# Polysketch attention with a gated causal layer: 64-column projection tiles, per-head gate weights, zero matmuls and a new order

## The chip, the cores and the metric

The kernel runs on one core of one Trainium2 chip. A core has five engines that matter here: TensorE (PE, matrix products, with a row of its own for the loads of its stationary operand, PEld), VectorE (DVE), ScalarE (ACT), GpSimd (POOL) and SyncE (SP, which here only starts DMA transfers). Each engine works through its own instructions in the order in which they were issued, and waits on semaphores for the others. The metric is the device time of one execution in microseconds (us), as the median of the runs shown.

## The reference

With batch 4, 4 heads, sequence length 1088, head size 32 and sketch size r = 8, inputs and output in float32:

```python
def phi(x):                                   # S1, S2: 8 x 32
    a = einsum('rd,bhsd->bhsr', S1, x)
    b = einsum('rd,bhsd->bhsr', S2, x)
    return einsum('bhsi,bhsj->bhsij', a, b)   # 64 features for each row
q_p, k_p = phi(q), phi(k)
kv  = einsum('bhsf,bhsd->bhfd', k_p, v)       # over the whole sequence
z   = sum(k_p, axis=2)
num = einsum('bhsf,bhfd->bhsd', q_p, kv)
den = einsum('bhsf,bhf->bhs', q_p, z) + 1e-6
x   = (num / den) with the heads side by side # 4 x 1088 x 128
gate_pre[s] = sum over t<5 of conv_w[t] * x[s - 4 + t]
out = (sigmoid(gate_pre) * (x @ w_val)) @ w_out
```

The output of a batch needs the kv and z of the batch's whole sequence, so k and v of a batch come before the second half of its q.

## The kernel before

**Tiling.** A batch's sequence is cut into three units of twelve tiles of 32 rows (the last unit is padded). With four batches that makes twelve units for k and twelve for q, numbered 0 to 11. A unit of k or q is loaded as 128 partitions (4 heads x 32 rows) by 384 columns; a 32x32-block transpose on DVE (`kT`, `qT`, lines 293 and 432) brings the head dimension onto the partitions.

**k side.** `k_ab` (line 302) projects a unit on TensorE: for each of three column blocks t and each of four quarters x, one float32 matmul whose stationary operand is a 128x32 quarter of kT and whose moving operand is S3, the block-diagonal S1 and S2 (64 columns). It writes 32 partitions of PSUM: a tile of 128 rows by 32 columns of the array. `k_cp` copies the result to SBUF, `k_phi` multiplies out the 64 features (three per unit, on POOL, some on DVE), and `k_kv` (line 330) multiplies them with v, four float32 matmuls of 32 columns for each t. z is not summed from the features: `k_z` multiplies the two projections with each other, `z_mask` masks them on DVE, and `z_c` turns the result into a vector c that stands as a third block of 32 columns in the moving operand of the q projection (`rhsq`), so that a.c summed over i gives the denominator.

**From kv to weights.** The kernel doesn't compute x. It folds kv into the two following products. `kv_cols` (line 385) copies kv from PSUM into two masked copies side by side (128 columns, float32), `kv_bf` casts these to bf16, `wg_mm` (line 404) multiplies a 64-row half of them with `dcw`, the convolution weights on a diagonal (5 x 64 columns), `wg_ev` casts the result to the bf16 gate weights, and `kw_mm`, `kw_ev` make the value weights kw = kv @ w_val likewise.

**q side.** `q_ab` (line 437) projects a unit with the same quarters as k, 96 moving columns. `q_cp`, `q_prod`, `q_den`, `q_rc`, `q_an` make the denominator, its reciprocal and the normalised a; `q_phi` multiplies out the features in bf16 on DVE; `q_pt` transposes them on TensorE through the one PSUM buffer of tag "pt", and `q_ev` copies them to phiT. `q_halo` copies a batch's last tiles, shifted by one position, ahead of its first ones, so that the five taps find the rows before them.

**Output side.** Thirteen groups of up to 384 positions: `g_mm` (line 521, five taps for each of two head pairs, 64-column tiles) gives gate_pre, `g_sig` the sigmoid on ACT, `g_val` the values, `g_gv` their product (DVE or POOL), `g_out` the product with w_out, `g_ev` its copy, `g_st` the stores on SP (four to six DMAs for a group up to group 8, one for each later group; the last one on ACT).

**Buffers.** PSUM: one buffer of tag "k" (k projections from unit 3 on, half of the gate weights, the value weights, a few small ones), two of "q", one of "kv", one of "pt", three of "g" (the first three k projections, the other half of the gate weights, all of the output side). In SBUF there are two buffers for k and for v; q has one for all batches, so a q load waits for the transpose of the same unit of the batch before.

**Order.** The loads of k and q of batch 0, k and v of batch 1 and 0, the two weights and v of batch 1 are issued first, on SP. Then the setup: three zero matmuls into `warm_ps`, identities, masks, S3, with two more zero matmuls (lines 170 to 236). Everything after is a list written out in `ORDER` (line 637): each word is a step of the table `STEPS`, with its unit or batch, and a letter V, A or P ahead of the dot picks DVE, ACT or POOL in place of the step's usual engine in `HOME`. Every instruction is kept in that order on its engine. So where a step stands in the list decides what it queues behind on each engine that it uses, SP included.

All of the program's instructions carry the line of the helper that pins them (line 72), so the profile is read by the names of tiles: `abk` and `abq` are the projections' PSUM tiles, `ab_sb` and `ac` their copies, `phik` and `phiq` the features, `kv` the accumulators, `wg_ps` and `kw_ps` the weights, `pt` the transposed features, `g_ps`, `v_ps`, `o_ps` the output side.

Of the kernel before, what the change touches and what calls it, by code (L numbers as in the profile page):

```python
# [16 lines left out]
def kernel(  # L17
# [24 lines left out]
    B, H, S, D = q.shape  # L42
    r = S1.shape[0]
    assert (B, H, S, D, r) == (4, 4, 1088, 32, 8)
    P = 128
    R2 = r * r
    HR = H * r
    J, NT, U, M4, NCK = 32, 34, 3, 4, 3
    TU = M4 * NCK
    TM = U * NCK  # L50
    W = TU * J
# [26 lines left out]
    def ctile(shape, dt, name):  # L78
        return const.tile(shape, dt, tag=name, name=name)
# [139 lines left out]
    w_out_sb = ctile([P, P], BF16, "w_out_sb")  # L219

    id64 = ctile([P, 2 * D], F32, "id64")
    cwt = ctile([P, KT], F32, "cwt")
    dcw = ctile([P, KT, 2 * D], F32, "dcw")

    POOL.memset(w_val_sb, 0.0)
    POOL.memset(q_sb[0][:, NT * D :], 0.0)
# [7 lines left out]
        )  # L234
    POOL.tensor_copy(out=s2x, in_=S3[:, 1].unsqueeze(1).to_broadcast([P, NCK, HR]))
    POOL.tensor_tensor(out=id64, in0=identf[:, : 2 * D], in1=identf[:, 2 * D :], op=ALU.add)
    def conv_weights():
        cw_ps = ps_k.tile([P, KT], F32, tag="k", name="cw_ps")
        PE.transpose(cw_ps, cw_nat, identf[:KT, :KT])
        SCA.copy(out=cwt, in_=cw_ps)  # L240
        POOL.tensor_mul(
            dcw, id64.unsqueeze(1).to_broadcast([P, KT, 2 * D]),
            cwt.unsqueeze(2).to_broadcast([P, KT, 2 * D]),
        )

    def weights():
# [10 lines left out]
    def fill_2():  # L257
        for b in range(B):
            POOL.memset(phiT[b][:, :, 0].rearrange("p g (T j) -> p g T j", j=J)[:, :, :, 0:1], 0.0)

    def pad_k():

        POOL.memset(k_sb[0][:, NT * D :], 0.0)
# [4 lines left out]
    def s_rhs(eng, b):  # L268
        copy(eng, out=rhsq[b][:, 0:2, :], in_=S3)

    def s_chunks():
        s2_ps = ps_k.tile([NCK * HR, P], F32, tag="k", name="s2_ps")
        PE.transpose(s2_ps, s2x.rearrange("p t x -> p (t x)"), identf)
        SCA.copy(out=s2t, in_=s2_ps)

    kv_ps = [None] * B
    wg = [None] * B
    wgp, kwp, kvx, kvt, zms = ({} for _ in range(5))
    kw = [None] * B
    n_kv = [0] * B  # L280
# [4 lines left out]
    def copy(eng, out, in_):  # L285
        (eng.copy if eng is SCA else eng.tensor_copy)(out=out, in_=in_)

    def quarter(xT, u, t, x):
        lo = u * W + t * P + x * J
        return xT[:, lo : lo + J]  # L290


    def k_T(i):
# [8 lines left out]
    def k_ab(i):  # L302
        b, u = divmod(i, U)
        pool, tag = (ps_g, "g") if i < U else (ps_k, "k")
        ab = pool.tile([P, 2, NCK, HR], F32, tag=tag, name="abk")
        for t in range(NCK):
            for x in range(M4):
                PE.matmul(
                    ab[J * x : J * (x + 1), :, t, :], lhsT=quarter(kT[b], u, t, x), rhs=S3,
                    start=True, stop=True,  # L310
                )
        abk[i] = ab
# [62 lines left out]
    def z_c(eng, b):  # L375
# [6 lines left out]
            )  # L382
        copy(eng, out=rhsq[b][:, 2, :], in_=c_ps)

    def kv_cols(eng, b):

        kvx[b] = work.tile([P, 2, R2], F32, tag="kvx", name="kvx")
        if eng is SCA:
            for x in range(2):
                SCA.activation(  # L390
                    out=kvx[b][:, x], in_=kv_ps[b][:, :R2], func=ACT.Identity, scale=m2[:, x : x + 1]
                )
            return
        DVE.tensor_mul(
            kvx[b],
            kv_ps[b][:, :R2].unsqueeze(1).to_broadcast([P, 2, R2]),
            m2.unsqueeze(2).to_broadcast([P, 2, R2]),
        )

    def kv_bf(eng, b):  # L400
        kvt[b] = work.tile([P, P], BF16, tag="kvt", name="kvt")
        copy(eng, out=kvt[b], in_=kvx[b].rearrange("p x f -> p (x f)"))

    def wg_mm(b, g):
        gs = slice(2 * D * g, 2 * D * (g + 1))
        pool, tag = (ps_k, "k") if g == 0 else (ps_g, "g")
        wgp[b, g] = pool.tile([P, KT, 2 * D], F32, tag=tag, name="wg_ps")
        PE.matmul(
            wgp[b, g], lhsT=kvx[b].rearrange("p x f -> p (x f)")[gs], rhs=dcw[gs], start=True, stop=True
        )  # L410

    def wg_ev(eng, b, g):
        if wg[b] is None:
            wg[b] = work.tile([P, 2, KT, 2 * D], BF16, tag="wg", name="wg")
        copy(eng, out=wg[b][:, g], in_=wgp[b, g])

    def kw_mm(b):
        kwp[b] = ps_k.tile([P, 2, P], F32, tag="k", name="kw_ps")
        PE.matmul(kwp[b], lhsT=kvt[b], rhs=w_val_sb, start=True, stop=True)

    def kw_ev(eng, b):
        kw[b] = work.tile([P, 2, P], BF16, tag="kw", name="kw")
# [8 lines left out]
    def q_ab(i):  # L431
        b, u = q_unit(i)
        ab = ps_q.tile([P, 3, NCK, HR], F32, tag="q", name="abq")
        for t in range(NCK):
            for x in range(M4):
                PE.matmul(
                    ab[J * x : J * (x + 1), :, t, :], lhsT=quarter(qT[b], u, t, x), rhs=rhsq[b],
                    start=True, stop=True,
                )
        abq[i] = ab  # L440
# [169 lines left out]
    def g_st(i):  # L610
# [14 lines left out]
        ldk=load_k, ldq=load_q, ldv=load_v, pad=pad_k, f1=fill_1, f2=fill_2, w=weights,  # L625
        cw=conv_weights, mz=mask_z, sr=s_rhs, s2=s_chunks,
        kT=k_T, kab=k_ab, kcp=k_cp, kp=k_phi, kkv=k_kv, kz=k_z, zm=z_mask, c=z_c,
        kvx=kv_cols, kvt=kv_bf, wgm=wg_mm, wge=wg_ev, kwm=kw_mm, kwe=kw_ev,
        qT=q_T, qab=q_ab, qcp=q_cp, qpr=q_prod, qden=q_den, qrc=q_rc, qan=q_an, qphi=q_phi,
        qpt=q_pt, qev=q_ev, halo=q_halo,  # L630
        val=g_val, gmm=g_mm, sig=g_sig, gv=g_gv, o=g_out, oev=g_ev, st=g_st,
    )
    HOME = dict(
        {n: SCA for n in ("kcp", "c", "kvt", "wge", "kwe", "qcp", "qev", "oev")},
        **{n: POOL for n in ("sr", "kp", "qpr", "qan", "halo")}, kvx=DVE, gv=DVE,
    )
# [30 lines left out]
    for step in ORDER.split():
        name, *where = step.split(".")
# [31 lines left out]
```

## Time and profile before

| what | us |
|---|---|
| median of three runs | 65.04 |
| lowest and highest | 64.75, 65.14 |
| the profiled execution's own time | 64.56 |
| its span, first to last instruction | 62.8 |
| TensorE busy in the span | 52.3 |
| VectorE busy | 43.8 |
| ScalarE busy | 32.5 |
| GpSimd busy | 32.2 |

The profiled execution's time holds some 1.8 us outside its span. Two passes of TensorE make one float32 matmul, so each of them stands in the trace as two records. Records of TensorE are pipelined and their ends are modelled: the time that a group of matmuls takes is read from its first start to the next group's first start. In the timeline's lines a matmul is given with its rows and columns of the array (128*32) and its moving operand (128x64).

Further times of single operations, as the groups of the same profile give them: a phik product on POOL 626 ns, a phiq product on DVE 948 ns, a copy of pt on ACT 806 ns and on DVE 534 ns, a kT transpose 631 ns in the mean, a copy of a projection on ACT about 320 ns, a cast of the gate weights on ACT 429 ns, the memset of `zeros` on DVE 272 ns.

### The profile page before, as it was taken

Reading aid. Unit: us, or ns where it says so; the run is one execution under the profiler, and the core shown is the slowest. Engines: PE = TensorE matmul, PEld = TensorE weight load, DVE = VectorE, ACT = ScalarE, POOL = GpSimd, SP = SyncE. Lnnn points to the kernel's source line nnn. Section 1 sums busy time; section 2 is a strip of 40 time slices with the busy share of each in tenths; the row PEclk is TensorE's granted clock in tenths of the full one; section 3 lists DMA queues with packets and bytes.
Section 4 is the critical chain, followed back from the end, with each engine's and each line's share of the span. In section 5 each row is a group of like instructions: output and inputs, shape, how many; then the busy total and the mean of one; then the engine's idle time right before and its main releaser. Section 6 shows DMA issues by size and latency. Waiting matters only on the chain.

```text
span 62.8 us, 3063 instructions
## 1 busy us (share of the span) xinstructions
PE 52.3 (83%) x1269; PEld 37.5 (60%) x1269; DVE 43.8 (70%) x118; ACT 32.5 (52%) x85; POOL 32.2 (51%) x84
## 2 busy tenths in 40 slices
PE   1977958998994998999799999979999998986100
PEld 0215828986683596685677867748894675562000
DVE  2267968392979899995999995972793599837000
ACT  0823221324883329675748686353958757856200
POOL 5555368797895997629629992524630040000000
PEclk9999999999999999999999999999999999999996
DMA  0499995999701799898384311403023224402280
GB/s 0 71 336 345 365 297 152 259 241 318 247 25 24 189 262 258 284 266 220 108 243 124 86 31 33 120 15 83 22 63 89 63 52 118 110 23 72 94 257 16
DMA packets 9256, 9.38 MB, mean 149 GB/s; under 512 B 1941, under 2 KB 9242, under 8 KB 9242
## 3 DMA queue, kind: packets, MB, share of 16 engines
q1 hardware_dynamic: 9072, 9.05, 50.1%
q8 instruction: 10, 0.16, 1.1%
q10 hardware_dynamic: 170, 0.13, 0.7%
q14 instruction: 4, 0.03, 0.2%
HBM read 6.95 MB, written 2.23 MB: 146 GB/s over the span
## 4 chain that ended last, share of the span: by engine, by line
PE 42%; DMA 20%; DVE 19%; ACT 4%; SPq 3%; issue 3%; POOL 1%; DVEq 0%; ACTq 0%
PE g_ps L72 8%; DMA k_sb<-in_k_dram 7%; PE kv L72 7%; PE abq L72 7%; DMA v_sb<-in_v_dram 6%; PE abk L72 6%; DVE gv L72 5%; DVE phiq L72 4%; DMA q_sb<-in_q_dram 4%; PE warm_ps L72 4%; SPq L72 3%; PE o_ps L72 3%; DVE kT L72 2%; DMA out_dram<-o_sb 2%; DVE o_sb L72 2%
## 5 line engine op out<-in xcount | busy, mean ns | idle before, releaser
L72 POOL TENSOR_TENSOR phik<-ab_sb 128x256 f32<-128x256 f32 x32 | 19.4, 626 | 3.0 <-ACT ab_sb L72 2.8
L72 DVE TENSOR_TENSOR phiq<-an,abq 128x768 bf16<-128x768 f32 (+2 forms) x13 | 11.3, 886 | 0.4
L72 PE MATMUL g_ps<-phiT,wg 128*64 128x384 bf16 (+3 forms) x130 | 11.1, 308 | 0.2 <-DVE rden L72 0.2
L72 PE MATMUL abq<-rhsq,qT 128*32 128x96 f32 x288 | 8.9, 268 | 0.5 <-ACT rhsq L72 0.3
L72 DVE STREAM_TRANSPOSE kT<-k_sb 128x384 f32<-128x384 f32 x12 | 7.3, 631 | 2.2 <-DMA k_sb<-in_k_dram 2.2
L72 PE MATMUL abk<-S,kT 128*32 128x64 f32 x288 | 7.9, 255 | 1.0 <-DVE kw L72 0.8
L72 PEld LDWEIGHTS <-wg 128*64 128x64 bf16 x130 | 7.5, 109 | 1.8 <-issue 0.5
L72 DVE TENSOR_TENSOR gv<-gate,v_ps 128x256 bf16<-128x256 bf16 (+3 forms) x14 | 6.1, 453 | 3.4 <-PE v_ps L72 1.5
L72 ACT COPY phiT<-pt 128x768 bf16<-128x768 bf16 (+1 forms) x10 | 7.8, 784 | 1.0 <-PE pt L72 0.8
L72 ACT ACTIVATE gate<-g_ps 128x384 bf16<-128x384 f32 (+3 forms) x13 | 5.8, 451 | 4.9 <-PE g_ps L72 3.7
L72 PE MATMUL kv<-phik,v_sb 128*32 128x64 f32 x288 | 7.2, 234 | 0.8 <-DVE rhsq L72 0.4
L72 PEld LDWEIGHTS abq<-rhsq,qT 128*32 128x32 f32 x288 | 7.0, 120 | 1.0 <-ACT rhsq L72 0.4
L72 ACT COPY ab_sb<-abk 128x192 f32<-128x192 f32 x11 | 3.6, 323 | 7.1 <-PE abk L72 6.2
L72 POOL TENSOR_TENSOR prod<-ac 128x96 f32<-128x96 f32 x7 | 2.7, 390 | 8.7 <-ACT ac L72 7.9
L72 PEld LDWEIGHTS abk<-S,kT 128*32 128x32 f32 x288 | 6.0, 132 | 2.0 <-DVE kw L72 1.0
L72 PEld LDWEIGHTS kv<-phik,v_sb 128*32 128x32 f32 x288 | 5.7, 119 | 1.7 <-issue 1.1
L72 DVE STREAM_TRANSPOSE qT<-q_sb 128x384 f32<-128x384 f32 x12 | 6.5, 555 | 0.1
L72 PE MATMUL pt<-identity,phiq 128*128 128x128 bf16 x72 | 6.2, 220 | 0.0
L72 PE MATMUL v_ps<-phiT,kw 128*128 128x384 bf16 (+3 forms) x26 | 5.9, 308 | 0.0
L72 ACT COPY o_sb<-o_ps 128x384 f32<-128x384 f32 (+3 forms) x12 | 4.7, 411 | 1.9 <-PE o_ps L72 1.9
L72 PEld LDWEIGHTS <-phiq 128*128 128x128 bf16 x72 | 4.7, 98 | 1.1 <-issue 0.3
L72 PE MATMUL o_ps<-w_out_sb,gv 128*128 128x128 bf16 (+1 forms) x37 | 4.6, 224 | 0.8 <-DVE gv L72 0.6
(74 smaller groups left out, 64.4 us busy)
## 6 DMA issues: line engine op xcount, KB each, us to landing
v_sb<-in_v_dram SPq DMA_DIRECT2D x15, 144.0 KB, 3.6
q_sb<-in_q_dram SPq DMA_DIRECT2D x8, 192.0 KB, 3.7
k_sb<-in_k_dram SPq DMA_DIRECT2D x7, 192.0 KB, 3.9
out_dram<-o_sb SPq DMA_DIRECT2D x24, 48.0 KB, 1.6
q_sb<-in_q_dram SPq DMA_DIRECT2D x4, 160.0 KB, 3.3
k_sb<-in_k_dram SPq DMA_DIRECT2D x3, 160.0 KB, 4.0
k_sb<-in_k_dram SPq DMA_DIRECT2D x1, 384.0 KB, 3.4
out_dram<-o_sb SPq DMA_DIRECT2D x12, 32.0 KB, 1.6
```

The lines of the kernel that those rows point to most:

```text
L72: return lambda *a, **k: tc.keep_in_program_order(call(*a, **k))
```

## The change

1. The projections take halves in place of quarters: two matmuls for each t with a stationary operand of 128x64, each writing 64 partitions. The moving operands stay.
2. The gate weights: `kv_copy` copies kv once, unmasked, in float32 (step `kvx`, usually on ACT); `wg_mm` makes all four heads in one step, each head a matmul of 32 rows and 64 columns with 5 x 32 moving columns, written to its own half of the partitions. `wg_ev` copies each head's result onto its place in `wg`, which now exists once for each batch and whose other places are zeroed by the new step `f3` (two DVE memsets for each batch). The masked copy is made in bf16 from kvx by `kv_cols` (step `kvt`) and serves the value weights alone. `dcw` is half as wide, with a new 32-column identity `id32`.
3. A step `wm`: one zero matmul of 512 or 256 columns into `warm_ps`. Six of them stand in the list: two after s2, one after cw, one after kz.0, one after kz.2, one after c.0.
4. A new order. Up to the first kkv steps it is, on TensorE, s2, wm.0, wm.1, kab.0, cw, wm.2, kz.0, wm.3, kab.1, kab.2, kz.1, kz.2, wm.4, c.0, wm.5, qab.0, qab.1, kab.3. The memsets f3.3 and f3.1 stand ahead of kT.0, f3.0 and mz ahead of kT.1, and f3.2 later. Several copies change their engine (all qev and kwe are on ACT after; wge.2.0 and wge.3.0 on DVE).

```diff
-    dcw = ctile([P, KT, 2 * D], F32, "dcw")
+    dcw = ctile([P, KT, D], F32, "dcw")
+
+    wg = [ctile([P, 2, KT, 2 * D], BF16, f"wg{b}") for b in range(B)]
...
+    POOL.tensor_tensor(out=id32, in0=id64[:, :D], in1=id64[:, D:], op=ALU.add)
...
+    def fill_3(eng, b):
+        for x in range(2):
+            eng.memset(wg[b][R2 * x : R2 * (x + 1), :, :, D * (1 - x) : D * (2 - x)], 0.0)
...
+    def work_on_zeros(_, n):
+        PE.matmul(warm_ps[:, :n], lhsT=zeros[:, :P], rhs=zeros[:, :n], start=True, stop=True)
...
-    def quarter(xT, u, t, x):
-        lo = u * W + t * P + x * J
-        return xT[:, lo : lo + J]
+    def half(xT, u, t, x):
+        lo = u * W + t * P + x * 2 * J
+        return xT[:, lo : lo + 2 * J]
...
-            for x in range(M4):
+            for x in range(2):
                 PE.matmul(
-                    ab[J * x : J * (x + 1), :, t, :], lhsT=quarter(kT[b], u, t, x), rhs=S3,
+                    ab[2 * J * x : 2 * J * (x + 1), :, t, :], lhsT=half(kT[b], u, t, x), rhs=S3,
                     start=True, stop=True,
                 )
...
+    def kv_copy(eng, b):
+        kvx[b] = work.tile([P, R2], F32, tag="kvx", name="kvx")
+        copy(eng, out=kvx[b], in_=kv_ps[b][:, :R2])
...
+    def wg_mm(b):
+
+        for g in range(2):
+            pool, tag = (ps_k, "k") if g == 0 else (ps_g, "g")
+            wgp[b, g] = pool.tile([P, KT, D], F32, tag=tag, name="wg_ps")
+            for x in range(2):
+                hs = slice(D * (2 * g + x), D * (2 * g + x + 1))
+                PE.matmul(
+                    wgp[b, g][R2 * x : R2 * (x + 1)], lhsT=kvx[b][hs], rhs=dcw[hs], start=True, stop=True
                 )
...
     def wg_ev(eng, b, g):
-        if wg[b] is None:
-            wg[b] = work.tile([P, 2, KT, 2 * D], BF16, tag="wg", name="wg")
-        copy(eng, out=wg[b][:, g], in_=wgp[b, g])
+        for x in range(2):
+            xs = slice(R2 * x, R2 * (x + 1))
+            copy(eng, out=wg[b][xs, g, :, D * x : D * (x + 1)], in_=wgp[b, g][xs])
...
+    s2 wm.0.512 wm.1.512 f3.3 f3.1 pad f1 kT.0 f3.0 mz kab.0 kcp.0 cw wm.2.512 kz.0 wm.3.256 kT.1
+    sr.0 kT.2 kab.1 kab.2 kp.0.0 kcp.1 srA.1 kz.1 kcp.2 kz.2 wm.4.256 qT.1 qT.0 zm.0 c.0 wm.5.256
+    kpV.2.2 kpV.0.2 qab.0 qab.1 kT.3 kT.5 qcp.0 kp.1.1 kp.1.2 kab.3 f2 qcp.1 kkv.1.2 kpV.2.1 kT.4
...
+    kp.3.2 qprV.2 kz.3 wgm.0 kz.4 kkv.5.0 kkv.3.1 kz.5 kkv.4.0 ldq.5 zm.1 wge.0.0 wge.0.1 kkv.5.1
+    kkv.3.0 qden.2 c.1 kwm.0 kwe.0 kT.6 qrc.2 qpt.1 kp.4.1 qev.1 qab.3 halo.0 ldk.3 qcp.3 kab.6
...
+    qan.7 qrc.8 qan.8 o.3 kp.9.2 val.4 o.1 st.2 qpt.6 qT.10 oev.3 kz.10 kp.11.0 kp.11.2 qphi.7
+    kkv.10.1 kkv.9.0 oev.1 kz.11 qev.6 kkv.9.2 qphi.8 kp.11.1 kkv.11.2 st.3 kkv.10.2 kkv.10.0
+    kkv.11.0 zm.3 kkv.9.1 c.3 gv.4 qT.9 kkv.11.1 val.5 kvtP.2 qpt.7 qab.10 qab.9 o.4 gv.5 qev.7
+    qcp.9 kvxV.3 kwm.2 qcpV.10 qpr.10 haloV.2 qpt.8 oev.4 o.5 qprV.9 qev.8 oev.5 kwe.2 qden.10
+    qden.9 qrc.10 qT.11 gmm.6 gmm.8 sig.6 sig.8 gmm.7 qan.10 qrc.9 wgm.3 sig.7 kvtA.3 val.7 val.6
...
+    gv.10 qpt.11.1 qev.11.1 st.8 gv.9 o.10 gmm.11 val.11 oev.10 gmm.12 sig.11 val.12 gv.11 st.10 o.9
+    sig.12 gv.12 o.11 oev.9 st.9 o.12 oev.12 oevV.11 st.11 st.12
```

The list is cut. In the new list qT.2 stands behind qphi.0, which moves it past many DVE steps; kwe.0 stands on ACT ahead of kT.6; ldk.3 stands behind halo.0, and ldq.8, ldq.6 and ldv.2 follow it.

## The prediction

> **What bounds the kernel now.** I read the page first, then a table by stage, then the chain of waits, then TensorE's timeline.
>
> ```profile
> PE 52.3 (83%) x1269; PEld 37.5 (60%) x1269; DVE 43.8 (70%) x118; ACT 32.5 (52%) x85; POOL 32.2 (51%) x84
> ```
>
> The averages mix stages, so the stretches follow (span's start to 62.8 us; busy time of each engine, with instructions).
>
> ```profile
> 4.80:11.60 6.80, 5.43 (x153) 4.57 (x156) 5.02 (x11) 1.77 (x7) 4.12 (x8) 1.00 0.88 283
> 11.60:19.80 8.20, 7.17 (x248) 5.66 (x238) 6.13 (x17) 4.55 (x12) 7.31 (x21) 1.00 0.66 194
> 19.80:45.00 25.20, 24.26 (x727) 18.15 (x727) 21.17 (x58) 14.95 (x42) 16.71 (x33) 1.00 0.53 147
> 45.00:55.50 10.50, 10.01 (x126) 6.80 (x125) 8.32 (x22) 7.46 (x17) 1.39 (x4) 1.00 0.29 77
> ```
>
> From 19.8 on TensorE (first number) is busy 96% of the time and VectorE 84%; the others have room. Before that there are round trips and loads. Three pieces of the chain of waits:
>
> ```profile
> 9.41 0.20 ACT rhsq L72
> 9.65 1.23 PE abq L72 x24
> ...
> 13.12 4.61 DMA k_sb<-in_k_dram
> ```
>
> The q projection starts at 9.65, when a row of round trips (copy, z matmuls, mask, c) has ended. Batch 2 of k lands at 17.74; SP issues loads without a pause up to 11.65, so that landing does not follow the compute.
>
> TensorE's timeline (start, duration, instruction) gives the prices:
>
> ```profile
> 12.21 0.87 PE L72 MATMUL abk<-S,kT 128*32 128x64 f32 x24
> ...
> 19.79 0.54 PE L72 MATMUL abk<-S,kT 128*32 128x64 f32 x24 [0.79 <-DVE kw L72]
> 20.26 0.50 PE L72 MATMUL v_ps<-phiT,kw 128*128 128x384 bf16 x2
> 20.69 1.00 PE L72 MATMUL g_ps<-phiT,wg 128*64 128x384 bf16 x10
> ...
> 24.96 0.81 PE L72 MATMUL wg_ps<-dcw,kvx 64*128 64x320 f32 x4
> 25.70 0.34 PE L72 MATMUL o_ps<-w_out_sb,gv 128*128 128x128 bf16 x3
> ...
> 32.05 0.50 PE L72 MATMUL v_ps<-phiT,kw 128*128 128x384 bf16 x2
> 32.39 0.50 PE L72 MATMUL pt<-identity,phiq 128*128 128x128 bf16 x6
> ...
> 34.38 0.52 PE L72 MATMUL abk<-S,kT 128*32 128x64 f32 x24
> 34.72 0.86 PE L72 MATMUL kv<-phik,v_sb 128*32 128x64 f32 x32
> ...
> 37.11 0.68 PE L72 MATMUL abq<-rhsq,qT 128*32 128x96 f32 x24
> 37.64 0.54 PE L72 MATMUL abk<-S,kT 128*32 128x64 f32 x24
> ...
> 42.05 0.77 PE L72 MATMUL kv<-phik,v_sb 128*32 128x64 f32 x40 [0.41 <-DVE rhsq L72]
> ```
>
> A k projection lasts 0.34 us (34.38 to 34.72), a q projection some 0.52. At 12.21 the next kv matmuls follow at 12.85, so 0.64: the array runs at half speed there, and only after some 13.8 us at full speed. The granted clock reads 1.00 in both stretches, so it doesn't show this. Two v_ps take 0.34 when the same tile shape follows (32.05 to 32.39) and 0.43 when another follows (20.26 to 20.69): 0.09 us per change of tile shape.
>
> **64-column tiles.** The 24 records of a k projection are 12 matmuls in two passes, four tiles side by side: 6 slots of 56 ns. With 64 columns there are 12 records, two tiles side by side: 6 slots again. q likewise. I cost this at nothing, if two loads of 64 columns fit behind a slot. No row has that load. wg_ps bounds it: two passes of 320 columns at 56 ns per 64 are 0.56, the drain 0.09, and it holds TensorE 0.74 (24.96 to 25.70), which leaves 0.09 for a load of 128 columns, some 45 to 50 ns for 64. The other end is two loads one after the other, 100 ns. I take 50, since the kernel's four loads of 32 columns do run together. Behind a slot of 56 it is just hidden; after a change of shape it stands bare, some 25 ns more than with 32 columns, about 12 times: +0.3.
>
> **Changes of shape.** Here a rule speaks against the change: the Trainium skill, TensorEngine Tiling (Array Packing), Key Properties, says that changing the tiling mode, not just the tile, drains the engine. Projections and kv matmuls (both 32 columns now) no longer share a shape. It gives no price; the row does, 0.09. The rule taken with only the projections' shape changed in the old order, I count 25 more switches, +2.2 us. Counting along the two orders as given: 40 before, 53 after, by stage 1 to 10 up to the first kkv, 6 to 11 up to kab.6, 23 to 22 up to gmm.6, 10 and 10 after. So +0.9 in the front, +0.5 in the second stage, -0.1 in the long one.
>
> **Gate weights.** Now 0.107 at most of load and two passes, 0.65 without the drain. After: four tiles at once, two passes of 160 columns, 2 x 0.14 and 0.05 of load: 0.33. Four times -0.32. If pairs run one after the other the saving is nil; I take the four at once, as the present two row tiles run together. wge becomes two copies of 64x160 each: a 128x320 cast is 429 ns, 128x192 copies 319, so 290 each and some 0.1 more per wge where they follow closely. The masked ACT pair (0.52) becomes one kvx copy (some 0.2) ahead of wgm; kvt falls off that path. POOL loses three kvt at 0.29; the half-width dcw saves about 0.3 there, id32 costs 0.2.
>
> **Front.** f3.3, f3.1 are four memsets ahead of kT.0. The zeros row is 272 ns for 256 words; these have 320 bf16, 160 words: 0.17 each, 0.33 if done by element. 0.7 to 1.3 in all; I take 0.7, the zeros row being in words. kT.0 then starts at about 4.1 instead of 3.9, kab.0 at 5.0 (4.82). cw and wm.2 (0.43 at half speed) and two drains put kz.0 at 6.5 (6.12); wm.3 and two more drains, kab.1 at 7.1 (6.25). Behind it wait kcp.1, kcp.2, zm, c and both q projections: qab at 10.3 (9.65), first kkv, with kab.3 moved ahead of it, at 12.9 (11.57): +0.7 like for like at half speed.
>
> Against that stands the clock. The Trainium skill, TensorE: Matmul & The Clock Gate, Part 1, says about 3.4 us of sustained activity in a free-running window releases the full rate. By that rule, with fillers from 4.0 on, release would come near 7.5 and give back kab.1 and kab.2 (0.7), both qab (0.9) and the kv and k work up to 13.8 (1.0). The row is less kind: in this run 7.0 to 10.4 was about 58% streaming and released nothing; 10.4 to 13.8, about 91%, did. With fillers I count some 80% from 3.6 to 7.0, then 61%. No run shows whether 80% is enough. Ends: nothing, or 2.5; I take release about 10.4, worth 1.2, so the front nets -0.5.
>
> **Up to kab.6.** kab.6 starts at 19.79, after 0.95 idle behind kweV.0, queued on DVE behind kT.6 and kT.7. After, kwe.0 is on ACT ahead of kT.6. From first kkv: 14 kkv 1.6, two each of kab, qab, qpt 2.4, small steps 0.9, eleven drains with loads 1.3: 6.2, so 18.5 to 19.6; the landing at 17.74 plus kT.6 (0.57) allows 18.4 at the earliest. I take 19.1: -0.7, which contains the front's part. SP: ldq.5 now waits for the later qT.2, with ldk.3, ldq.8, ldq.6 and ldv.2 queued behind it; the DMAs were idle from 17.3 to 20.4, so that is covered to about 17.
>
> **kab.6 to gmm.6.** 25.2 before. Five kkv now lie earlier (-0.56), two wgm -0.64, drains -0.1, bare loads +0.3. The waits after c (30.48 and 42.05, 0.5 to 0.6 each), where kkv followed c at once: after c.1 and c.2 other work follows, after c.3 not: -0.5. DVE loses two qev, kwe, an oev and three kp (about 4.0) and gains f3.2, copies and products (about 1.5); ACT gains some 2.3 (60% to 73%), POOL some 1.3. With these queues denser, new waits of 0 to 1.5: I take 0.7, half, as no row tells. Sum -0.8.
>
> **Tail.** gmm.6 onward is nearly the same: wgm.3 -0.32; o.9, for which gmm.11 waited 0.4, goes behind val.12. But SP issues 24 stores of 0.42 us almost without pause from 45 to 57.9, and the last three behind them. I take -0.2.
>
> Sum: -0.7 - 0.8 - 0.2 = -1.7. The profiled execution took 64.56 (span 62.8 and 1.8 around it), so 62.9; the median shown is 0.48 above it: **63.3 us**.
>
> **Rivals and chances.**
> (a) Forecast, 62.3 to 64.3: 0.49.
> (b) Release near 7 us and no new waits: -0.6 more at kab.6 (stopped by the landing), -0.7 in the long stage: 62.0. For it the 80%. 0.13.
> (c) The fillers do not do what they are for and the waits are at their upper end: +0.5 and +0.8 on (a): 64.6, no change. 0.16.
> (d) Slower: loads of two 64-column tiles don't run together. A slot becomes 100 instead of 56 for k and 83 for q: 72 x 44 + 72 x 17 ns = 4.4 us, minus 1.7: 67.7. It decides from a slot of 80 (72 x 24 = 1.7). Against it: today's loads overlap. 0.08.
> (e) Slower: the window falls badly. TensorE works without gaps from some 10.3; with a free window of 3.4 us the release can come as late as two windows on, 17.1, and half of 6.8 us, 3.4, is lost against (a). kab.6 then starts near 21.8 instead of 19.1: 66.0. It decides from kab.6 at 20.8. Against it: the runs shown lie within 0.4 us of each other, though the window would fall anew in each. 0.14.
>
> About 1% is what this kernel's measurement can tell from no change: 64.4 to 65.7. Faster 0.62, which is (a) and (b); same 0.16, (c); slower 0.22, (d) and (e). The range 61.3 to 66.4 takes in the middle of (b) and (e) and leaves out (d), half of (e)'s upper side and the edge of (b): under 2 in 10.
>
> **What would show it.** wg_ps near 0.42 from its start to the next matmul; abk still 0.34 from 12 records; abk at half speed only before about 10.4; kab.6 near 19.1; gmm.6 near 43. It is wrong if abk's slots exceed 56 ns, if kab.1 is later than 7.5 while the array stays slow to 13.8, or if new idle before pt, abk and kv in 19 to 43 is over 1.5 us.

## The result, and the profile after

The changed kernel took 62.05 us in the median of four executions (61.43 to 63.13), against 64.90 (64.70 to 65.14) before, next to it on the same chip: a ratio of 0.948, with a 95% interval of 0.941 to 0.954. The forecast was 63.3. Faster was right, but the gain is some 2.85 us where 1.7 were forecast. The profiled execution took 61.57 us with a span of 59.9. (All ratios in this text leave out executions more than 1.5% above their kernel's fastest.)

The page of the changed kernel: first the engines' busy time, then the queue that fetches instructions (packets, MB, share), then the shares of the chain of waits.

```profile
PE 50.7 (85%) x1003; PEld 36.2 (60%) x1003; DVE 44.3 (74%) x127; ACT 34.7 (58%) x96; POOL 31.8 (53%) x81
...
q8 instruction: 8, 0.13, 0.9%
...
PE 60%; DVE 15%; ACT 8%; issue 4%; POOL 4%; DVEq 0%; ACTq 0%
```

Before, the last of these lines read

```profile
PE 42%; DMA 20%; DVE 19%; ACT 4%; SPq 3%; issue 3%; POOL 1%; DVEq 0%; ACTq 0%
```

The loads, a fifth of the chain before, are gone from it, and TensorE has gone from 42% to 60%. The prediction did not ask for that; the last experiments below bear on where it comes from.

The table by stage, with the stages cut at the same steps as before (first kkv at 11.2, kab.6 at 17.9, gmm.6 at 42.5):

```profile
4.80:11.20 6.40, 5.77 (x106) 4.14 (x105) 5.54 (x15) 1.79 (x8) 4.58 (x17) 1.00 0.95 312
11.20:17.90 6.70, 6.39 (x212) 5.14 (x211) 5.95 (x19) 4.74 (x16) 6.58 (x15) 1.00 0.92 268
17.90:42.50 24.60, 23.10 (x543) 17.88 (x539) 20.37 (x57) 16.59 (x45) 16.54 (x31) 1.00 0.47 137
```

| stretch, us | before | after | difference | forecast |
|---|---|---|---|---|
| start to kab.6 | 19.8 | 17.9 | -1.85 | -0.7 |
| kab.6 to gmm.6 | 25.2 | 24.6 | -0.6 | -0.8 |
| gmm.6 to the end | 17.8 | 17.3 | -0.4 | -0.2 |

So it is the stretch before kab.6 that was missed. TensorE's timeline after (start, duration, instruction, records) shows why:

```profile
5.19 0.91 PE L72 MATMUL abk<-S,kT 128*64 128x64 f32 x12 [0.19 <-DVE kT L72]
6.03 0.27 PE L72 MATMUL cw_ps<-identf,cw_nat 5*128 5x5 f32 x1
6.23 0.59 PE L72 MATMUL warm_ps<-zeros 128*128 128x512 bf16 x1
6.74 0.27 PE L72 MATMUL kv<-ab_sb 128*32 128x1 f32 x8
6.94 0.28 PE L72 MATMUL warm_ps<-zeros 128*128 128x256 bf16 x1
7.16 0.92 PE L72 MATMUL abk<-S,kT 128*64 128x64 f32 x24
...
9.74 1.21 PE L72 MATMUL abq<-rhsq,qT 128*64 128x96 f32 x24 [0.18 <-ACT rhsq L72]
10.75 0.55 PE L72 MATMUL abk<-S,kT 128*64 128x64 f32 x12
11.22 0.54 PE L72 MATMUL kv<-phik,v_sb 128*32 128x64 f32 x24
```

kab.0 at 5.19 takes 0.91, half speed. kab.1 and kab.2 together, 24 records from 7.16, take 0.92: full speed. The array's clock was released in between: the trace's own clock record has full rate from 6.66 on, some 7 us earlier than before (13.82), and both q projections take 1.0 us instead of 1.9. The forecast had put the release at 10.4.

### The profile page after: what moved, and what is told of

It reads as the page before. It is cut to its first block, busy times and chain, and to the rows that moved or that the text cites. A ratio compares the mean times of both kernels' runs of the same rounds, so it can differ in the third digit from the quotient of the medians.

```text
span 59.9 us, 2553 instructions
## 1 busy us (share of the span) xinstructions
PE 50.7 (85%) x1003; PEld 36.2 (60%) x1003; DVE 44.3 (74%) x127; ACT 34.7 (58%) x96; POOL 31.8 (53%) x81
## 4 chain that ended last, share of the span: by engine, by line
PE 60%; DVE 15%; ACT 8%; issue 4%; POOL 4%; DVEq 0%; ACTq 0%
PE kv L72 12%; PE g_ps L72 11%; PE abq L72 10%; PE abk L72 7%; PE v_ps L72 5%; PE pt L72 5%; PE warm_ps L72 4%; DVE gv L72 4%; DVE wg L72 3%; POOL phik L72 3%; PE wg_ps L72 2%; PE o_ps L72 2%; DVE o_sb L72 2%; ACT wg L72 2%; DVE kT L72 1%
## 5 line engine op out<-in xcount | busy, mean ns | idle before, releaser
L72 POOL TENSOR_TENSOR phik<-ab_sb 128x256 f32<-128x256 f32 x33 | 19.9, 629 | 0.3 <-ACT ab_sb L72 0.3
L72 DVE TENSOR_TENSOR phiq<-an,abq 128x768 bf16<-128x768 f32 (+2 forms) x13 | 11.2, 881 | 0.1
L72 ACT COPY phiT<-pt 128x768 bf16<-128x768 bf16 (+2 forms) x13 | 9.7, 753 | 1.9 <-PE pt L72 1.7
L72 PE MATMUL abq<-rhsq,qT 128*64 128x96 f32 x144 | 7.7, 251 | 0.2 <-ACT rhsq L72 0.2
L72 PE MATMUL kv<-phik,v_sb 128*32 128x64 f32 x288 | 6.7, 223 | 1.1 <-DVE zm L72 0.6
L72 PE MATMUL abk<-S,kT 128*64 128x64 f32 x144 | 6.8, 234 | 0.2 <-DVE kT L72 0.2
L72 PEld LDWEIGHTS abq<-rhsq,qT 128*64 128x64 f32 x144 | 6.3, 136 | 0.8 <-POOL phiT L72 0.3
L72 PEld LDWEIGHTS abk<-S,kT 128*64 128x64 f32 x144 | 5.6, 144 | 1.7 <-DVE kT L72 1.1
L72 PE MATMUL warm_ps<-zeros 128*128 128x512 bf16 (+1 forms) x11 | 5.0, 529 | 1.3 <-DVE hm L72 1.3
L72 PEld LDWEIGHTS kv<-phik,v_sb 128*32 128x32 f32 x288 | 4.8, 109 | 2.1 <-DVE zm L72 0.9
```

The costliest lines, as they stand in the source:

```text
L72: return lambda *a, **k: tc.keep_in_program_order(call(*a, **k))
```

## Experiments

Besides the ratios, each kernel's profile gives the start of four steps; "full" is the release, where the clock record of the trace begins to read full rate. All times in us, one execution for each line.

| kernel | zero matmuls | full | first kkv | kab.6 | gmm.6 | span |
|---|---|---|---|---|---|---|
| before | 0 | 13.8 | 11.6 | 19.8 | 45.0 | 62.8 |
| changed kernel | 6 | 6.7 | 11.2 | 17.9 | 42.5 | 59.9 |
| changed, again (e5) | 6 | 4.9 | 11.3 | 18.4 | 42.6 | 60.2 |
| changed, third time (e9) | 6 | 14.1 | 13.5 | 20.2 | 44.5 | 61.4 |
| changed, first two zeros only (e10) | 2 | 14.1 | 13.1 | 20.0 | 44.3 | 62.3 |
| changed, no zeros (e1) | 0 | 15.9 | 13.1 | 20.8 | 45.0 | 62.7 |
| changed, 32 columns (e4) | 6 | 5.5 | 11.0 | 18.7 | 44.7 | 62.0 |
| changed, 32 columns again (e11) | 6 | 4.7 | 11.3 | 21.4 | 46.7 | 64.6 |
| old order, zeros (e2) | 6 | 5.0 | 10.6 | 19.9 | 45.6 | 63.5 |
| old order, 64 columns (e3) | 0 | 15.4 | 11.9 | 20.3 | 46.5 | 64.2 |
| old order, new gate weights (e6) | 0 | 13.1 | 11.5 | 19.6 | 48.0 | 65.6 |
| old order, zeros, kwe.0 on ScalarE (e7) | 6 | 7.6 | 10.8 | 18.8 | 46.6 | 64.4 |
| old order, zeros, 64 columns, kwe.0 on ScalarE (e12) | 6 | 5.8 | 10.8 | 17.8 | 44.8 | 61.6 |
| changed, order moved again (e8) | 7 | 7.1 | 11.3 | 18.2 | 42.6 | 60.6 |

### The zero matmuls

Theory A: the gain before kab.6 is the early release. The rival: it comes from the new order and the 64-column tiles.

**e1: the changed kernel without its zero matmuls.**

```diff
-    s2 wm.0.512 wm.1.512 f3.3 f3.1 pad f1 kT.0 f3.0 mz kab.0 kcp.0 cw wm.2.512 kz.0 wm.3.256 kT.1
-    sr.0 kT.2 kab.1 kab.2 kp.0.0 kcp.1 srA.1 kz.1 kcp.2 kz.2 wm.4.256 qT.1 qT.0 zm.0 c.0 wm.5.256
+    s2 f3.3 f3.1 pad f1 kT.0 f3.0 mz kab.0 kcp.0 cw kz.0 kT.1
+    sr.0 kT.2 kab.1 kab.2 kp.0.0 kcp.1 srA.1 kz.1 kcp.2 kz.2 qT.1 qT.0 zm.0 c.0
```

> The changed kernel without its six zero matmuls (wm steps left out of the order, nothing else; the result is the same). Theory A (the gain over the forecast comes from the array reaching full speed near 7.2 instead of 13.8 us, and the zero matmuls bring that): kab.1 and kab.2 run at half speed (a k projection 0.64 and not 0.35), full speed only somewhere between 10.4 and 14, and the time is 0.8 to 2.0 us above the changed kernel's 61.5. Theory B (the gain is the order's; the front is covered by the loads of batch 2): within 0.3 us of 61.5 either way, kab.6 still near 18.

64.23 us (63.04 to 64.45); before on that chip 65.71 (64.47 to 67.78). The timeline of e1 has the same steps at half speed:

```profile
6.83 1.70 PE L72 MATMUL abk<-S,kT 128*64 128x64 f32 x24
...
10.30 2.19 PE L72 MATMUL abq<-rhsq,qT 128*64 128x96 f32 x24 [0.40 <-ACT rhsq L72]
12.24 0.89 PE L72 MATMUL abk<-S,kT 128*64 128x64 f32 x12
13.06 0.87 PE L72 MATMUL kv<-phik,v_sb 128*32 128x64 f32 x24
```

Full speed comes at 15.9 and kab.6 at 20.8, 2.8 after the changed kernel's and 1.0 after the old one's. So the whole gain before kab.6 hangs on the early release, which is missing without the zeros. But the time stays below the kernel before, so the rest of the change does bring something, later.

**e2: the old order with the six zero matmuls**, at places like those of the changed kernel.

```diff
-    s2 f1 kT.0 cw kT.1 kab.0 srA.0 kcp.0 pad kz.0 kab.1 kT.2 kab.2 mz qT.1 kcp.1 qT.2 kcp.2 kp.0.2
-    kp.2.0 qT.0 kz.1 kz.2 zm.0 c.0 qab.1 kp.1.2 kp.2.2 kp.1.1 qab.0 kkv.1.2 qcp.1 ldq.3 qpr.1
+    s2 wm.0.512 wm.1.512 f1 kT.0 cw kT.1 kab.0 wm.2.512 srA.0 kcp.0 pad kz.0 wm.3.256 kab.1 kT.2 kab.2 mz qT.1 kcp.1 qT.2 kcp.2 kp.0.2
+    kp.2.0 qT.0 kz.1 kz.2 wm.4.256 zm.0 c.0 wm.5.256 qab.1 kp.1.2 kp.2.2 kp.1.1 qab.0 kkv.1.2 qcp.1 ldq.3 qpr.1
```

> The kernel before with the six zero matmuls at the corresponding places of its own order (two after s2, one each after kab.0, kz.0, kz.2 and c.0). Theory A: full speed by 7 to 11 us, and 0.8 to 1.6 us faster than before (63.3 to 64.1), less than that if kab.6 still waits for kweV.0 and the k load at 17.7. Theory B: the same as before or up to 0.4 slower, since two matmuls of 0.43 push kab.0 back by about 0.35.

65.44 us (64.49 to 67.84), ratio 0.995 (0.987 to 1.003): no change. Yet the release came at 5.0, and kkv started 1.0 earlier. The timeline of e2 shows where that went:

```profile
10.59 0.28 PE L72 MATMUL kv<-phik,v_sb 128*32 128x64 f32 x2
11.87 0.31 PE L72 MATMUL kv<-phik,v_sb 128*32 128x64 f32 x4 [1.01 <-DMA v_sb<-in_v_dram]
```

TensorE, now early, stands for v, and again at kab.6 for kw (1.0 us, kweV.0 in VectorE's queue, as before the change). In the old order an early clock alone is worth nothing that these runs can tell.

**e5 and e9: the changed kernel again, on two chips; e10: it with the first two zero matmuls only.**

```diff
-    s2 wm.0.512 wm.1.512 f3.3 f3.1 pad f1 kT.0 f3.0 mz kab.0 kcp.0 cw wm.2.512 kz.0 wm.3.256 kT.1
-    sr.0 kT.2 kab.1 kab.2 kp.0.0 kcp.1 srA.1 kz.1 kcp.2 kz.2 wm.4.256 qT.1 qT.0 zm.0 c.0 wm.5.256
+    s2 wm.0.512 wm.1.512 f3.3 f3.1 pad f1 kT.0 f3.0 mz kab.0 kcp.0 cw kz.0 kT.1
+    sr.0 kT.2 kab.1 kab.2 kp.0.0 kcp.1 srA.1 kz.1 kcp.2 kz.2 qT.1 qT.0 zm.0 c.0
```

> The changed kernel itself, to stand beside the other runs on one chip. Earlier runs: without its zero matmuls 62.7 us span (kab.6 at 20.8), with 32-column tiles 62.0 (kab.6 at 18.7). If both parts are needed, this run has kab.6 near 18, gmm.6 near 42.5, a span near 60, and no halt of TensorE over 0.4 us that has no wait behind it. If the earlier differences were the chip's, the span is 62 or more here.

> The changed kernel once more, so that the three others stand beside it on one chip. Both theories expect 62 to 62.6 us and a ratio to the kernel before of 0.95 to 0.96. Theory A (the gain sits in an early release of the clock, and the new order and the 64-column tiles let what follows use it) expects full speed from between 5.2 and 7.2, first kkv near 11.3, kab.6 near 18.0 to 18.4 and gmm.6 near 42.6.

> The changed kernel with the first two of the six zero matmuls (3.94 to 5.0 in its trace) and without the four later ones; the result is the same. If what counts is the stretch up to some 5.2, which in this form is filled as before, full speed comes by 5.2 and the time is that of the changed kernel within 0.5 us (62 to 63). If the later ones are needed, because the stretch that counts can fall on 5 to 9, full speed comes as late as in the changed kernel without any (15.9), kab.6 starts near 20.7 and the time is some 64.5. If it depends on where a window falls in an execution, single times scatter between these two, by 2 us or more.

e5: 63.13 us (61.97 to 64.17) against 65.05, ratio 0.959 (0.953 to 0.965). e9: 62.75 (62.02 to 63.77) against 65.76, ratio 0.953 (0.941 to 0.966). e10, on e9's chip: 63.81 (63.35 to 64.24), ratio 0.978 (0.967 to 0.988). The profiled execution of e9 took 63.13 us. Its timeline:

```profile
6.24 0.61 PE L72 MATMUL warm_ps<-zeros 128*128 128x512 bf16 x1
6.77 0.34 PE L72 MATMUL kv<-ab_sb 128*32 128x1 f32 x8
7.04 0.39 PE L72 MATMUL warm_ps<-zeros 128*128 128x256 bf16 x1
7.37 1.55 PE L72 MATMUL abk<-S,kT 128*64 128x64 f32 x24
...
10.69 2.19 PE L72 MATMUL abq<-rhsq,qT 128*64 128x96 f32 x24
12.64 0.88 PE L72 MATMUL abk<-S,kT 128*64 128x64 f32 x12
13.45 0.84 PE L72 MATMUL kv<-phik,v_sb 128*32 128x64 f32 x24
14.23 0.57 PE L72 MATMUL abk<-S,kT 128*64 128x64 f32 x12
```

Up to 6.2 this execution is the same as the first profile to 0.02 us, with the same zeros, and then the release does not come: it comes at 14.1. In all profiles, with zeros or without, it fell at 4.7 to 7.6 or at 13.1 to 15.9, and never between. With at least six zeros it was early in eight of nine profiles; with none or two, late in five of five. The 14 executions of the changed kernel lie between 61.4 and 64.2 (median 62.7); e5 (61.97 us) and the first profile (61.57 us) are early, e9 late, so a late release fits much of that scatter, though only three of the 14 were profiled.

**What decides.** The clock records of the traces show it. They begin at the release, which is why the stage tables print 1.00 ahead of it as well. In each of the 14 profiles every stretch at full rate lasts a whole number of steps of 3.413 us: 51.20 us in the first profile is 15 of them, 44.37 in e9 is 13. So the clock changes only at the end of such a step, and counting back from the release tells where the steps of an execution lie. They lie differently each time: one ended at 6.66 in the first profile, at 7.31 in e9. From the starts and columns of the matmul records I estimate in what share of each step TensorE was streaming (at half rate 512 columns of zeros take 0.43 us in these traces). In every step that ended with a release it was at least 75%; in every step at half rate that ended without one, at most 70%. The first profile's step up to 6.66 has 77%. In e9 the steps that end at 7.31 and 10.72 have 69% and 63%, and the one that ends at 14.13 has 95%.

Slid along e9's trace, a step finds its 71 to 75% early, by some 7.0, in 76 to 87 of 100 positions and otherwise only at 13.6 to 14.4. In e10's trace it does so early in 41 to 58 of 100, in e1's and in the kernel before in none. (These are estimates, from one trace each.) So six zeros make an early release likely, not certain. e10's profile can't show that the first two zeros are too few: its steps lay as e9's did (14.12 and 14.13), where six didn't do either.

Two sizes follow. On one chip, the four later zeros take the median from 63.81 to 62.75, of a gain of 3.0 in all, and the ratio from 0.978 to 0.953: a third to a half of the gain. Each of these medians mixes early and late releases in a share that isn't known. The rest is there with a release at 14.1: e10's profile has kab.6 at 20.0, no earlier than before, but only 24.3 us from there to gmm.6 in place of 25.2, and e1's has the same 24.3.

### The 64-column tiles

Theory A: they cost nothing, as forecast. The rivals: each change of shape costs 0.09 us, 2.2 in the old order; or they matter for something else.

**e3: the old order with 64 columns. e4 and e11: the changed kernel with 32 columns.** e3's edit; e4 and e11 have its reverse.

```diff
-            for x in range(M4):
+            for x in range(2):
                 PE.matmul(
-                    ab[J * x : J * (x + 1), :, t, :], lhsT=quarter(kT[b], u, t, x), rhs=S3,
+                    ab[2 * J * x : 2 * J * (x + 1), :, t, :], lhsT=half(kT[b], u, t, x), rhs=S3,
```

> The kernel before with 64-column projections alone, in its own order. By the forecast's prices: 65 changes of tile shape instead of 40, 25 x 0.09 = +2.2 us and bare loads +0.5, so 66.5 to 67.6; k slots 56 to 59 ns. Rival: most of the switches fall where TensorE waits anyway, 65.0 to 65.6. Rival: two loads don't run together, slots of 100 ns, over 69.

> The changed kernel with the projections back in 32-column tiles (everything else as changed). 49 changes of shape instead of 53, slots 56 instead of 58.5 ns: by these prices 0.3 to 0.6 us less TensorE time, so 60.9 to 61.5 if TensorE bounds; the tiles of 64 columns are then worth nothing. Rival: half the records are worth something in themselves (issue, weight loads), then above 62.2.

> The changed kernel with the projections in four 32-column tiles, as before, on the same chip as the changed kernel. Theory A (64-column tiles pay by halving the records that have to be fetched): 1.5 to 2.5 us above the changed kernel, 64 to 64.8, with halts of TensorE of 0.4 us or more and no recorded wait that end about 1.3 us after a packet of its instruction queue. Theory B (the tiles cost nothing and bring nothing, as forecast, and the halts seen in the earlier run were chance): within 0.5 us of the changed kernel, 62 to 63.

e3: 65.65 us (64.74 to 66.93), ratio 1.006 (0.995 to 1.017). From kab.6 to gmm.6 it takes 26.2 in place of 25.2, with 37 changes of shape in place of 25: 12 times 0.09 is the 1.0. (The new order has 25 there.) Before kab.6, 9 more changes cost 0.5 in the profile. The 2.2 that the rule alone would give in the old order is too much: the spans differ by 1.4, the medians by nothing that the interval can tell.

With 32 columns the changed kernel takes 65.94 us (63.74 to 66.41) in e4 and 65.99 (64.05 to 66.45) in e11, against 62.75 on e11's chip. The cleanest comparison is that of early releases: e4's profiled execution took 63.74, those of the changed kernel 61.57 and 61.97. TensorE's timeline of e4:

```profile
14.30 0.24 PE L72 MATMUL kv<-ab_sb 128*32 128x32 f32 x8
14.47 0.49 PE L72 MATMUL wg_ps<-dcw,kvx 32*64 32x160 f32 x4
15.82 0.49 PE L72 MATMUL wg_ps<-dcw,kvx 32*64 32x160 f32 x4 [0.86 <-issue]
```

and of e11, on another chip:

```profile
15.32 0.24 PE L72 MATMUL kv<-ab_sb 128*32 128x32 f32 x8
15.49 0.49 PE L72 MATMUL wg_ps<-dcw,kvx 32*64 32x160 f32 x4
17.35 0.49 PE L72 MATMUL wg_ps<-dcw,kvx 32*64 32x160 f32 x4 [1.38 <-issue]
```

TensorE stops in the middle of the gate weights, and "issue" says that nothing which the profile knows was waited for. In the records of the instruction queue a 16 KB packet ends at 14.49 in e4 and at 15.98 in e11, so 1.33 and 1.37 us before the stop ends. The other stops of this kind are the same: e4 at 20.12 (packet 18.80) and 33.56 (32.22), e11 at 35.62 (34.17). They add up to 2.2 us in e4 and 2.5 in e11, counted from the start of the last instruction before each. The changed kernel has one in each early profile, of 0.5 to 0.6: at 19.81 (packet 18.44) and, in e5, at 14.75 (13.16). I read this as instructions that are not there yet: with 32 columns a projection has twice the records, TensorE at full speed passes through its code faster, and the fetch falls behind. The page of e4 counts 10 packets, that of the changed kernel 8:

```profile
q8 instruction: 10, 0.16, 1.1%
```

That the fetch is the cause is not shown. It rests on this timing; no run changed the fetch alone, and most packets end without a stop behind them. The old order with 32 columns and an early release, which waits more for other things, has no such stop in e2 and one of 0.2 in e7.

Nor are these stops all of e11's 3.2 us in the median. Its profile also stood 0.9 for v at 12.6, and then the granted clock fell, as the page's row shows (40 slices of the span, in tenths of full speed):

```profile
PEclk9999999999965799999999999999999999999995
```

The clock record has half rate from 18.38 to 21.79, one step of 3.41 us, behind a step that held the long stop and in which TensorE was streaming for an estimated 43%. From the kkv steps at 18.75 to gmm.0 at 22.02 e11 takes 3.27 us, e4 1.94 for the same (17.22 to 19.16): 1.3 lost. e4's three slower executions (65.6 to 66.4 us) have mean granted clocks of 0.92 to 0.95, its profiled one 0.985, so such steps can be part of their time; they have no profile.

### The gate weights

**e6: the kernel before with the new gate weights alone**, with f3 spread over VectorE's queue and kvx and kvt on the engines of before.

```diff
-            wgp[b, g], lhsT=kvx[b].rearrange("p x f -> p (x f)")[gs], rhs=dcw[gs], start=True, stop=True
+                    wgp[b, g][R2 * x : R2 * (x + 1)], lhsT=kvx[b][hs], rhs=dcw[hs], start=True, stop=True
```

> The kernel before with the new gate weights alone (kvx copy, four row tiles of 32, two copies each, f3 memsets spread over idle stretches of DVE), 32-column projections, the old order. By the forecast's price: wg_ps from its start to the next matmul 0.42 to 0.45 instead of 0.74, four times -0.3; 0.6 to 1.2 us faster than before if TensorE bounds everywhere after 19.8, at most 0.3 of it lost to the longer wge. Rival: the saving disappears in later waits, within 0.3 us of before.

66.8 us (64.92 to 67.97) against 65.05: no gain, and rather slower; its fastest execution is where the kernel before is. The step is as cheap as forecast: 0.43 in its chain of waits, 0.74 before. But in the profiled execution (67.27 us, so not the fastest) the chain goes through loads:

```profile
24.63 0.17 SPq L72
...
25.80 5.13 DMA k_sb<-in_k_dram
...
31.05 0.58 DVE kT L72
31.63 0.08 DVE zm L72
...
31.75 0.31 PE kv L72 x8
```

The k load of batch 3 was issued from 24.84 (23.21 before) and landed at 30.93; kT.9 waited for it on VectorE, zm.2 behind kT.9, and TensorE stood 2.0 us for zm. The step that holds most of this wait was streaming for an estimated 39%, and behind it the clock was at half from 33.62 to 37.04:

```profile
PEclk9999999999999999999975799999999999999996
```

The work from 32.91 to 37.44 takes 4.53 us, the same work before 2.99 (30.92 to 33.91). In the old order the saving is worth less than where this load falls.

### What the old order lacks

**e7: e2 with kwe.0 on ScalarE. e12: e7 with 64 columns**, so everything but the gate weights and the new order.

```diff
-    qprV.2 ldq.7 c.1 kwm.0 sr.1 kweV.0 kp.4.0 qpt.1 qden.2 qev.1 kp.4.2 qab.3 kab.6 val.0 kp.5.2
+    qprV.2 ldq.7 c.1 kwm.0 sr.1 kwe.0 kp.4.0 qpt.1 qden.2 qev.1 kp.4.2 qab.3 kab.6 val.0 kp.5.2
```

> The kernel before with the six zero matmuls (as in the second run) and kwe.0 on ACT in place of DVE. The zeros alone gave full speed at 5.3 us, first kkv at 10.6, but then 1.2 us of waiting for v and 1.2 before kab.6 for kweV.0. If kweV.0 is what takes the lead back: kab.6 near 18.8 instead of 19.9, gmm.6 near 44.5, about 0.8 to 1.1 us faster than the run with zeros alone. If the loads hold it anyway: kab.6 after 19.3, within 0.4 us of it.

> The old order with the six zero matmuls, the 64-column tiles and kwe.0 on ScalarE, but with the old gate weights: all parts but those and the new order. Theory A (the old order has no use for an early release, since loads and VectorE's queue set the pace behind it): first kkv near 10.8 with about 1.2 of waiting for v behind it, kab.6 at 18.8 to 19.5, gmm.6 at 44.5 to 46.5, 64 to 65.5 us. Theory B (each part brings its own share and the shares add up): kab.6 near 18.0 and 62.5 to 63.3 us.

e7: 65.03 us (64.19 to 66.36), ratio 0.990 (0.987 to 0.994). e12: 65.03 (63.93 to 65.97) against 65.76, beside e9's 62.75. Both bring kab.6 forward, e12 to 17.8, ahead of the changed kernel (18.8 to 19.5 and 1.2 us of waiting for v were expected; v was there in time). And both lose the lead up to gmm.6: 27.8 and 27.0 us in place of 25.2, where the changed kernel needs 24.6. The waits of e12 on VectorE and TensorE, from 14 and from 17.9 on (sum, times, longest):

```profile
DVE kT L72 <- DMA k_sb<-in_k_dram: 2.0, 2, 1.4
...
PE abq L72 <- DVE phiq L72: 0.6, 1, 0.6
PE kv L72 <- DVE rhsq L72: 0.4, 1, 0.4
PE kv L72 <- POOL phik L72: 0.4, 1, 0.4
```

VectorE waits for k loads: 2.0 here, 2.6 in e7, 3.3 in e6, 1.2 before, 0.6 in e2, and not at all in e3 and in the changed kernel from 14 to 46. There SP issues the k load of batch 3 from 14.64 on, between two q loads:

```profile
11.34 2.31 SPq L72 DMA_DIRECT2D k_sb<-in_k_dram  x3
13.69 0.91 SPq L72 DMA_DIRECT2D q_sb<-in_q_dram  x2
14.64 1.38 SPq L72 DMA_DIRECT2D k_sb<-in_k_dram  x3
```

Before, the same load was issued at 23.21. I read this as what the new order gives: loads far ahead of their transposes, and 12 changes of shape fewer with 64 columns than the old order would have. The second is counted. The first is argued: no run moved these loads alone, and e3 shows that the old order doesn't always wait for them.

**e8: the changed kernel with one more zero matmul and kkv steps moved into the gaps behind zm and c.**

```diff
-    s2 wm.0.512 wm.1.512 f3.3 f3.1 pad f1 kT.0 f3.0 mz kab.0 kcp.0 cw wm.2.512 kz.0 wm.3.256 kT.1
+    s2 wm.0.512 wm.1.512 wm.6.256 f3.3 f3.1 pad f1 kT.0 f3.0 mz kab.0 kcp.0 cw wm.2.512 kz.0 wm.3.256 kT.1
...
-    kkv.11.0 zm.3 kkv.9.1 c.3 gv.4 qT.9 kkv.11.1 val.5 kvtP.2 qpt.7 qab.10 qab.9 o.4 gv.5 qev.7
+    kkv.11.0 kkv.9.1 kkv.11.1 zm.3 gv.4 val.5 c.3 qT.9 kvtP.2 qpt.7 qab.10 qab.9 o.4 gv.5 qev.7
```

> The changed kernel with three edits: one more zero matmul (256) after wm.1; in batch 1 the last two kkv go ahead of zm.1, and kwm.0, qpt.1 ahead of c.1, kab.6 ahead of qab.3; in batch 3 kkv.9.1 and kkv.11.1 go ahead of zm.3, and val.5 ahead of c.3. In the changed kernel TensorE stands 0.47 at 16.0, 0.47 at 38.3 and 0.57 at 39.2 for the mask and the copy of c. If TensorE bounds, 0.6 to 1.2 us faster than the changed kernel; rival: the waits only move to qab.3 and qab.10, within 0.3 us of it.

62.33 us (61.81 to 62.97), ratio 0.956 (0.952 to 0.960), beside e5's 0.959 on the same chip: no better. gmm.6 starts at 42.56, as in e5 (42.62); the waits moved elsewhere.

## Why the prediction was right and wrong

**Clock release: the step that failed.** "I take release about 10.4, worth 1.2, so the front nets -0.5." That was a value between two ends, and the runs show only the ends: 4.7 to 7.6, or 13.1 to 15.9. The free window of 3.4 us was right; what failed was to weigh its two outcomes into one time. "No run shows whether 80% is enough" has its answer, too: the first profile's window streamed for an estimated 77%, and that was enough, where 70% was not. With an early release kkv starts at 11.2 (-0.35) and kab.6 at 17.9 to 18.4 (-1.85 and -1.4, not -0.7). With a late one, e9, kkv is at 13.5 and kab.6 at 20.2, +0.4. The forecast of 63.3 is near what a late execution takes (63.13 in e9), and the rule's end (near 7.5) gives the recorded result. Taking a middle here described no execution at all; two cases with a chance for each would have. The sum of 6.2 from first kkv to kab.6 was short as well: it took 6.7, and 7.1 in e5.

**The landing.** That "the landing at 17.74 plus kT.6 (0.57) allows 18.4 at the earliest" was wrong too, and held rival (b) back at kab.6. SP issued this load from 11.34 in place of 12.18, as one v issue ahead of it was shorter, and kT.6 ran at 16.51, right behind zm and den in VectorE's queue, with no wait for the load. SP's issues without a pause showed that the landing did not follow the compute. They didn't show that it stays at 17.74.

**Rivals.** (b) named 62.0 for a release near 7 us and got the time, with a chance of 0.13, though its long stretch did not shrink by the further 0.7. (e), the window that falls badly, happens in some executions, with a release at 14.1, two windows past 7.31, rather than 17.1. (d) is refuted: twelve records of a k projection take 0.35 in the chain of waits (18.11), so two loads of 64 columns do run beside the slots. (c) is refuted in part: zeros do help, in this order; in the old one (e2) they don't.

**64-column tiles at nothing.** Their price was right, 0.35 for 0.34, and so was 0.09 for a change of shape at full speed (e3). What they save was missed: 2553 instructions against 3129 with 32 columns (e4), and 1.6 to 2 us fewer of the stops once the array is fast.

**Gate weights.** 0.42 forecast, 0.43 measured in the chain:

```profile
14.87 0.50 PE L72 MATMUL wg_ps<-dcw,kvx 32*64 32x160 f32 x8
15.30 0.23 PE L72 MATMUL kv<-ab_sb 128*32 128x32 f32 x3
```

from 14.87 to 15.30. A copy of wge takes 0.28 on ScalarE and 0.32 on VectorE, where 0.29 was forecast.

**kab.6 to gmm.6.** -0.8 forecast, -0.6 in the first profile and -0.9 in e5 and e9. TensorE is busy 1.16 less there (23.10 for 24.26; the sum of kkv, wgm, drains and loads was 1.0) and idle 0.56 more (1.50 for 0.94; 0.2 was forecast). Right in sum; that no transpose waits for a k load there any more was not seen.

**Tail.** -0.2 forecast, -0.4 measured, within the 0.7 by which tails of the same kernel differ (17.3, 17.6 in e5, 16.9 in e9).

**Front.** The four memsets took 0.19 each (0.17 forecast), kab.0 started at 5.19 (5.0), kab.1 at 7.16 (7.1).

## What to carry to other kernels

Where a clock is released or not by how a window falls, forecast two cases and give each a chance; a value between them describes no execution. The chance can be worked out: slide the window along the trace and count the positions in which it is dense enough. Ask of a faster front what it will run into: the same zeros were worth nothing in an order whose loads and queues kept the old pace, and some third to half of the gain in one that had moved its loads 8 us ahead. And count instructions as well as slots: a tile shape that streams the same columns with half the records can win time that no busy row shows.

## What the runs showed of the hardware

- The TensorE clock changed only on a grid of 3.413 us that lies differently in each execution: all full stretches in the 14 traces are whole multiples of it. At half rate, steps with TensorE streaming for an estimated 75% or more ended with a release; none with 70% or less did. With the same zero matmuls at the same moments, to within 0.02 us, the release came at 6.66 in one execution and at 14.13 in another.
- Once released, the clock can fall again: one step at half followed a step with an estimated 43% of streaming in e11 and 39% in e6 (1.3 and 1.5 us lost). Steps with an estimated 43 to 47% in e2 and e4 kept full rate, so where it falls is not settled.
- TensorE can stop for 0.2 to 1.4 us with no wait recorded, and such a stop ended 1.26 to 1.6 us after a 16 KB packet of its instruction queue (all nine found, in e4, e5, e6, e7, e11 and the changed kernel). That the packet is the cause is not shown.
- A change of tile shape costs 0.09 us at full speed and about 0.14 at half, in e3's trace: 152 ns from the last start of abk to the first of kv, less a slot of 58, and 244 ns less a slot of 107.
